# VectorE block transposes for p, score tiles of 256 columns, and V loaded in runs of eight keys per partition

## The chip, the cores and the metric

The kernel runs on one core of one Trainium2 chip. The metric is the device time of one execution in microseconds. Of seven executions of the kernel before in one set of rounds, six took 309.45 to 313.45 us; the seventh took 314.72, over 1.5% above the fastest, and such a one counts as slow. Ratios below are the mean time of one kernel's fast runs over the mean time of the fast runs of the kernel before in the same rounds, so they are not quite the ratio of the medians that are quoted beside them.

## The reference, cut to what matters

Two layers of attention over a window of 2048 cached keys, each followed by a gated feed-forward block, for 4 tokens with one query each. There are 16 query heads on 8 K/V heads of 256 dimensions. Both layers read the same caches.

```python
x = A_x                                          # 4 tokens x 448
x = x + attention(layernorm(x), k_cache, v_cache, wq, wo)
x = x + ffn(layernorm(x), w_gate, w_up, w_down)
x = x + attention(layernorm(x), k_cache, v_cache, wq, wo)
x = x + ffn(layernorm(x), w_gate, w_up, w_down)
return x
# in attention, per token and per K/V head: two queries q (2 x 256), keys K and values V (2048 x 256)
#   p = softmax(q @ K.T / 16);  o = p @ V
```

K and V of one token and head are 1 MB each, as bf16. The kernel splits each into two halves of 512 KB. Some halves are kept on the chip from the first layer for the second; all others are loaded twice.

## The kernel before

It is written as a graph of operations. The kernel's own scheduler puts them in order for the five engines from a plan (the order of heads, and offsets for the loads). These are the parts that the change and the argument touch.

```python
# loads: one DMA per half, each to all 128 partitions
ksrc = A_k_cache[t, kvh, s0:s0 + WIN, :].rearrange("(p j) d -> p (j d)", p=128)
e.dma_start(half[cell[0]][:, :], ksrc[:, 2048 * hf:2048 * hf + 2048])          # K: 8 keys, 4096 bytes a run
...
vsrc = A_v_cache[t, kvh, s0:s0 + WIN, :].rearrange("(a q g) d -> q a g d", a=4, q=128)
e.dma_start(half[cell[0]][:, :].rearrange("p (a g d) -> p a g d", a=2, g=4),
            vsrc[:, 2 * hv:2 * hv + 2, :, :])                                  # V: 4 keys, 2048 bytes a run
...
# K is turned in place by VectorE; its rows are taken as 32 groups of 32 pairs of bf16
a = half[cell[0]][:, :].bitcast(UINT32).rearrange("p (k s) -> p k s", k=32)
e.transpose(a, a)
...
# scores of a single group: a tile of 128 columns; two heads may share a group, with 256 columns
for ce in range(8):
    for hf in range(2):
        for x in range(2):
            qd = 64 * hf + 32 * x                    # 8 rows in one of the four quarters of 32 rows
            e.matmul(Sb[s_][qd:qd + 8, 0:128], lhsT=qe[...], rhs=kt[...], ...)
...
# p = exp(scores) is turned by TensorE (matmuls with selectors) and copied to bf16 by ScalarE
e.matmul(o, lhsT=praw[0:R, c0:c0 + 128], rhs=w, ...)
e.activation(pf, Yb[p_][:, 0:PW], ACT.Copy)
```

The row of q that multiplies a key is masked by the quarter of K's partitions in which the key stands. So a key's place in K's load fixes its quarter and column in the score tile. The turn of p then fixes the partition in which V's row for that key must be.

Of the kernel before, what the change touches and what calls it, by code (L numbers as in the profile page):

```python
# [5 lines left out]
ACT = mybir.ActivationFunctionType  # L6
# [7 lines left out]
B = 4  # L14
D = 448
# [11 lines left out]
KEEP_K = (6, 5, 6, 6)  # L27
KEEP_V = (5, 4, 3, 3)


KLEAD = 3.2
KTAIL = -1.1
VLAG = 0.4
SLEAD = 0.7
FR = 7.5
FRD = 10.1
WOR = -8.6
CROSS = 10
# [9 lines left out]
    ("k", 0, 0, 0): -4, ("k", 0, 0, 1): -0.5, ("k", 0, 0, 2): -1.5, ("k", 0, 0, 3): 1, ("k", 0, 0, 4): -3,  # L48
    ("k", 0, 0, 5): -0.5, ("k", 0, 0, 6): -1.5, ("k", 0, 1, 2): -0.5, ("k", 0, 1, 3): 0.5, ("k", 0, 1, 5): 2,
    ("k", 0, 1, 6): -4, ("k", 0, 1, 7): -3, ("k", 1, 0, 1): 2.5, ("k", 1, 0, 2): -3, ("k", 1, 0, 3): -0.5,  # L50
    ("k", 1, 0, 4): 2, ("k", 1, 0, 5): -0.5, ("k", 1, 0, 6): -1, ("k", 1, 1, 0): 2, ("k", 1, 1, 1): -2,
    ("k", 1, 1, 3): -4.5, ("k", 1, 1, 4): -2, ("k", 1, 1, 5): 0.5, ("k", 1, 1, 7): -3, ("k", 2, 0, 0): 2,
    ("k", 2, 0, 1): 0.5, ("k", 2, 0, 3): -1, ("k", 2, 0, 4): 2, ("k", 2, 0, 6): 2, ("k", 2, 0, 7): 0.5,
    ("k", 2, 1, 0): -2.5, ("k", 2, 1, 1): 2, ("k", 2, 1, 2): -3, ("k", 2, 1, 4): 1, ("k", 2, 1, 5): 4.5,
    ("k", 2, 1, 6): 2, ("k", 3, 0, 1): 0.5, ("k", 3, 0, 2): 3, ("k", 3, 0, 3): -1, ("k", 3, 0, 4): 1,
    ("k", 3, 0, 6): 1, ("k", 3, 1, 0): 1, ("k", 3, 1, 1): 1.5, ("k", 3, 1, 2): -6, ("k", 3, 1, 4): -1,
    ("k", 3, 1, 6): 6.5, ("k", 3, 1, 7): -4, ("v", 0, 0, 2): -2, ("v", 0, 0, 3): 0.5, ("v", 0, 0, 5): -2.5,
    ("v", 0, 0, 6): 0.5, ("v", 0, 0, 7): 1.5, ("v", 0, 1, 0): 2, ("v", 0, 1, 1): -2.5, ("v", 0, 1, 2): 3,
    ("v", 0, 1, 3): -1, ("v", 0, 1, 4): -3, ("v", 0, 1, 6): -0.5, ("v", 0, 1, 7): -3, ("v", 1, 0, 0): 3,
    ("v", 1, 0, 2): 1, ("v", 1, 0, 3): 0.5, ("v", 1, 0, 4): 4, ("v", 1, 0, 5): 1.5, ("v", 1, 0, 6): 2,  # L60
    ("v", 1, 0, 7): 1, ("v", 1, 1, 1): 2, ("v", 1, 1, 2): -3, ("v", 1, 1, 3): -1, ("v", 1, 1, 5): 0.5,
    ("v", 1, 1, 6): 0.5, ("v", 1, 1, 7): 2, ("v", 2, 0, 0): 2, ("v", 2, 0, 1): -1, ("v", 2, 0, 2): 3,
    ("v", 2, 0, 4): 1, ("v", 2, 1, 1): -3.5, ("v", 2, 1, 2): -1, ("v", 2, 1, 3): 6, ("v", 2, 1, 5): -2,
    ("v", 2, 1, 6): 1.5, ("v", 3, 0, 0): 2.5, ("v", 3, 0, 2): 1, ("v", 3, 0, 3): 1, ("v", 3, 0, 4): 1.5,
    ("v", 3, 0, 7): 1.5, ("v", 3, 1, 2): -1, ("v", 3, 1, 5): 1, ("v", 3, 1, 7): 0.5,
}
PLAN = (
    "001", "003 005", "002", "007", "004 006", "000", "100 102", "106", "017", "014 016", "101+104", "012+107",
    "105 103", "207", "010", "201", "015 301", "013", "202+117", "113", "204+205", "114 200", "011", "203", "206",
    "115 111", "112", "110", "116 300", "305 210", "307", "304+213", "303", "302", "216 306", "212 217", "215 214",  # L70
    "316+313", "211", "311+314", "310+312", "315+317",
# [8 lines left out]
TARGET = 4000  # L80
WINDOW = 3.41
HOLD = 7
HOLD_MIN = 0.8
# [27 lines left out]
class Op:  # L111
    __slots__ = ("i", "eng", "dur", "rank", "emit", "deps", "succ", "nbytes", "dsem", "dval",
                 "start", "end", "pos", "waits", "inc", "val", "known", "run", "cell", "rel", "bank")

    def __init__(self, i, eng, dur, rank, emit):
        self.i, self.eng, self.dur, self.rank, self.emit = i, eng, dur, rank, emit
        self.deps = {}
        self.succ = []
        self.nbytes = 0
        self.dsem = None  # L120
        self.dval = 0
        self.cell = None
        self.rel = ()
        self.bank = ()
        self.inc = False
        self.val = 0
        self.waits = []


class Graph:  # L130
# [42 lines left out]
    def dma(self, rank, nbytes, emit, sem, r=(), w=(), run=8192, cell=None):  # L173

        o = self.op(SP, 0.05, rank, emit, r=r, w=w)
        o.run = run
        o.nbytes = nbytes
        o.cell = cell
        if cell is None:
            self._count(o, sem)  # L180
        return o

    def _count(self, o, sem):
        o.dsem = sem
        self.dcount[sem] = self.dcount.get(sem, 0) + 16
        o.dval = self.dcount[sem]


    def schedule(self, npool):
# [16 lines left out]
        pe_end = 0.0  # L206

# [15 lines left out]
        while n < len(self.ops):  # L223
# [16 lines left out]
            if o.cell is not None:  # L240

                slot = min(pool)
# [15 lines left out]
            if e == PE:  # L258
                at = pe_end
                while t - at >= FILLD + 0.02:  # L260
                    bank = None
                    if at >= FILL0 and sum(c for b, c in busy[-24:] if b > at - WINDOW) < TARGET:
# [88 lines left out]
    def emit(self, eng_name, eng, sems, dsems):  # L351
        for o in self.order[eng_name]:
# [6 lines left out]
            if o.dsem is not None:  # L359
                ins.then_inc(dsems[o.dsem], 16)  # L360
            elif o.inc:
                ins.then_inc(sems[eng_name], 1)
# [9 lines left out]
def build(nc, A_x, A_k_cache, A_v_cache, A_wq, A_wo, B_x, B_w_gate, B_w_up, B_w_down, out):  # L372
# [3 lines left out]
    with ExitStack() as es:  # L376
# [14 lines left out]
        selt = [sb(f"selt{h}", [128, 4, 12], BF16) for h in range(2)]  # L391
        sel1 = [sb(f"sel1{h}", [128, 2, 4, 2, 2], BF16) for h in range(2)]
        small = sb("small", [128, 17 + 2 * NS + 8 * NY + 2 * B], FP32)
        onesf, wrow, lomask, expo = small[:, 0:1], small[:, 1:5], small[:, 5:6], small[:, 6:11]
# [3 lines left out]
        fars = small[:, 11:14].bitcast(BF16)  # L398
        far, far1 = fars[:, 0:4].rearrange("p (P o n) -> p P o n", P=2, o=1), fars[:, 4:6].rearrange("p (o n) -> p o n", o=1)
# [5 lines left out]
        qe = [sb(f"qe{i}", [128, 2, 8, 4, 2], BF16) for i in range(NQ)]  # L405
# [11 lines left out]
        xb = wideb[:, 0:4 * B].rearrange("p (c t) -> p c t", t=B)  # L417
        hT = wideb[:, 512:576]
        qS = wideb[:, 0:128]
        praw = sb("praw", [128, 514], BF16)  # L420
        pT = [sb(f"pT{s}", [128, 4, 4, 12], BF16) for s in range(NP)]
# [27 lines left out]
        def c_fill(e):  # L449
            e.memset(onesf[:, :], 1.0)  # L450
            e.memset(expo[:, 0:1], -0.5)
            e.memset(expo[:, 1:5], -1.0)
# [15 lines left out]
        for a in range(4):  # L468
            g.op(DVE, 0.1, R0, lambda e, a=a: e.memset(qmask[32 * a:32 * a + 32, a:a + 1], DH ** -0.5), r=("qmask",),
                 w=(f"qmask{a}",))  # L470
        ivq = identb[:, :].rearrange("p (q z n) -> p q z n", q=4, n=2)
        for h in range(2):
            g.op(DVE, 0.1, R0, lambda e, h=h: e.memset(selt[h][:, :, :], 0.0), w=(f"selt{h}",))
            for P in range(2):
                for y in range(2):
                    c0 = 8 * P + 2 * y
                    g.op(DVE, 0.1, R0, lambda e, h=h, P=P, c0=c0: e.tensor_copy(
                        selt[h][:, :, c0:c0 + 2], ivq[:, 2 * P + h, 0:4, :]), r=("identb",), w=(f"selt{h}",))
# [8 lines left out]
        for P in range(2):  # L487
            g.op(DVE, 0.1, R0, lambda e, P=P: e.tensor_scalar(
                far[:, P, 0, :], nmask[:, 2 * P:2 * P + 2], negm[0][:, 1:2], FAR,
                op0=ALU.add, op1=ALU.mult), r=("rs0", "negm0"), w=("far",))  # L490
# [6 lines left out]
        ivt = identb[:, :].rearrange("p (h x z n) -> p h x z n", h=2, x=2, n=2)  # L497
        for h in range(2):
            for y in range(2):
                for x in range(2):  # L500
                    g.op(DVE, 0.1, R0, lambda e, h=h, y=y, x=x: e.tensor_copy(sel1[h][:, x, :, y, :], ivt[:, h, x, 0:4, :]),
                         r=("identb",), w=(f"sel1{h}{y}{x}",))
        for s_ in range(NS):
            g.op(DVE, 0.2, R0, lambda e, s_=s_: e.memset(Sb[s_][:, :], 0.0), w=(f"s{s_}",), bank=(f"S{s_}",))
        g.op(DVE, 0.2, R0, lambda e: e.memset(praw[:, :], 0.0), w=("praw",))
# [47 lines left out]
        def norm(t, rank, x):  # L553
# [15 lines left out]
            vec(rank, lambda e: e.tensor_copy(s[:, 12:14], Z2[:, 0:2]), ("z2",), (k + "m",), 0.14, ("Z2",))  # L569

# [7 lines left out]
            def gp(emit, r, w, dur=0.25):  # L578
                g.op(POOL, dur, rank, emit, r=r, w=w)
            gp(lambda e: e.tensor_scalar(s[:, 15:16], s[:, 12:13], s[:, 12:13], -1e-5, op0=ALU.mult, op1=ALU.add),  # L580
               (k + "m",), (k + "e",))
            gp(lambda e: e.tensor_scalar(s[:, 5:6], s[:, 13:14], s[:, 15:16], None, op0=ALU.subtract),
               (k + "m", k + "e", k + "w", k + "v"), (k + "h",))
            gp(lambda e: e.tensor_tensor(s[:, 8:9], s[:, 5:6], expo[:, 0:1], op=ALU.pow), (k + "h", "expo"), (k + "r2",), 0.58)

        def rowvec(dst, key, ts, rank):
            for i, t in enumerate(ts):
                if i == 0:
                    g.op(POOL, 0.27, rank, lambda e, t=t: e.tensor_tensor(
                        dst, rmask[:, t:t + 1], st[:, t, 8:9], op=ALU.mult), r=("rmask", f"st{t}r2"), w=(key,))  # L590
                else:
                    g.op(POOL, 0.27, rank, lambda e, t=t: e.tensor_scalar(
                        dst, rmask[:, t:t + 1], st[:, t, 8:9], dst, op0=ALU.mult, op1=ALU.add),
# [6 lines left out]
        def qproj(ts, rank):  # L600
# [3 lines left out]
            rowvec(rvec[:, 0:1], "rvq", ts, rank)  # L604
# [52 lines left out]
        def ffn_row(ts, rank):  # L657
            rowvec(rvec[:, 1:2], "rvf", ts, rank)
            g.op(POOL, 0.27, rank, lambda e: e.tensor_single_scalar(rvec[:, 2:3], rvec[:, 1:2], 0.5, op=ALU.mult),
# [506 lines left out]
```

## Time and profile before

| | before |
|---|---|
| time, median of 2 runs | 312.48 us (312.2 to 312.75) |
| bytes loaded | 107.25 MB: 94 MB in 98 loads of V and 82 of K, the rest weights |
| last bytes | about 294 us; the tail after them 19 us |
| VectorE busy | 198.1 us (63%) |

The prediction below reads this profile and shows the lines that carry the reading. In them PE is TensorE and PEld its weight loads, DVE is VectorE, ACT ScalarE, POOL GpSimd, and SPq the queue of SyncE, which issues the loads. PEclk is the clock granted to TensorE (1.00 or 9 is full). wq and wo are the weights of attention, wg, wu and wd those of the feed-forward block; `half` is a buffer for half of K or V, S a score tile. Here are only the groups that the change replaces: the line in the program, engine, operation, output and input, count, then busy us and mean ns of one, then the engine's idle time ahead of them and what ended it.

```profile
L853 DVE STREAM_TRANSPOSE half<-half 128x1024 uint32<-128x1024 uint32 x82 | 100.3, 1230 | 3.3 <-DMA half<-in_A_k_cache_dram 3.0
...
L883 PE MATMUL S<-half,qe 128*8 128x128 bf16 x1472 | 30.6, 222 | 7.7 <-issue 3.6
...
L907 DVE TENSOR_REDUCE tiny<-S 104x1 bf16<-104x128 f32 (+1 forms) x55 | 16.8, 306 | 22.8 <-PE S L883 17.5
...
L929 ACT ACTIVATE praw<-S,small 104x128 bf16<-104x128 f32 x46 | 16.8, 365 | 55.5 <-DVE small L921 54.7
...
L951 ACT ACTIVATE pT<-Y 128x64 bf16<-128x64 f32 (+1 forms) x55 | 13.2, 240 | 20.7 <-PE Y L943 17.6
```

K's transposes (L853) are half of VectorE's work, and stay. The score matmuls (L883), the row maximum (L907) and the exponential (L929) work on 128 columns in a single group. The ScalarE copy of the turned p (L951) goes.

### The profile page before, as it was taken

How to read it: one execution, taken by the hardware profiler on the slowest of the kernel's cores; microseconds unless marked ns; L12 is line 12 of the kernel's file. 1: busy time of each engine (PE TensorE's matmuls, PEld its weight loads, DVE VectorE, ACT ScalarE, POOL GpSimd, SP SyncE). 2: the span in 40 equal slices, each digit the busy share in tenths (PEclk: the TensorE clock that was granted, in tenths of full speed). 3: DMA queues.
4: the chain of work that ended last, by engine and by line, in shares of the span. 5: the costliest groups of instructions: out<-in, count | busy, mean ns of one | idle time of the engine just before them, and what ended most of it. 6: DMA issues, size and time to landing. Idle time of an engine off the chain costs nothing.

```text
span 313.2 us, 11054 instructions
## 1 busy us (share of the span) xinstructions
PE 255.0 (81%) x4814; PEld 129.5 (41%) x4814; DVE 198.1 (63%) x627; ACT 68.1 (22%) x196; POOL 87.1 (28%) x236
## 2 busy tenths in 40 slices
PE   4788777869598867898988785988969779888996
PEld 1323323424123543264444252544435444445563
DVE  8527945845114995559778565699776656585532
ACT  0030010303003121143322032203403231423310
POOL 1521011303202322134342031441505133332530
PEclk9999999999959997799999997589999986999995
DMA  7999999999999999999999999779999998999500
GB/s 275 317 394 401 403 401 393 397 391 346 271 387 343 306 409 393 386 340 383 397 400 394 398 395 393 281 254 374 383 334 369 391 394 314 300 387 390 206 2 3
DMA packets 45024, 107.25 MB, mean 342 GB/s; under 512 B 3240, under 2 KB 8880, under 8 KB 44592
## 3 DMA queue, kind: packets, MB, share of 16 engines
q1 hardware_dynamic: 44976, 106.55, 92.9%
q8 instruction: 38, 0.62, 0.8%
q14 instruction: 10, 0.08, 0.1%
HBM read 106.53 MB, written 0.00 MB: 340 GB/s over the span
## 4 chain that ended last, share of the span: by engine, by line
PE 37%; DMA 26%; DVE 15%; SPq 14%; issue 4%; ACT 3%; POOL 1%; DVEq 0%; ACTq 0%
DMA half<-in_A_v_cache_dram 13%; DMA half<-in_A_k_cache_dram 9%; DVE half L853 7%; PE Y L973 7%; PE A L1098 7%; SPq L848 6%; SPq L527 6%; PE S L883 5%; DMA wu_sb<-in_B_w_up_dram 4%; SPq L861 3%; PE A L1026 2%; DVE oh L990 2%; PE Z L617 2%; PE Y L943 2%; PE Y L996 1%
## 5 line engine op out<-in xcount | busy, mean ns | idle before, releaser
L853 DVE STREAM_TRANSPOSE half<-half 128x1024 uint32<-128x1024 uint32 x82 | 100.3, 1230 | 3.3 <-DMA half<-in_A_k_cache_dram 3.0
L1098 PE MATMUL A<-identb,small 128*128 128x512 bf16 x249 | 83.1, 435 | 0.0
L986 POOL TENSOR_TENSOR small<-small 128x2 f32<-128x2 f32 (+1 forms) x55 | 41.3, 753 | 62.1 <-DVE small L964 59.6
L973 PE MATMUL Y<-half,pT 128*4 128x256 bf16 (+1 forms) x1024 | 46.4, 283 | 10.7 <-DMA half<-in_A_v_cache_dram 6.5
L900 POOL TENSOR_TENSOR qe<-qc,tiny 128x64 bf16<-128x64 bf16 x64 | 18.3, 293 | 83.0 <-PE S L883 61.6
L988 ACT ACTIVATE oh<-Y 128x256 bf16<-128x256 f32 x55 | 21.1, 384 | 83.0 <-PE Y L973 71.9
L990 DVE SCALAR_TENSOR_TENSOR oh<-oh,small,Y 128x256 bf16<-128x256 bf16 x55 | 25.9, 470 | 19.0 <-ACT oh L988 18.5
L883 PE MATMUL S<-half,qe 128*8 128x128 bf16 x1472 | 30.6, 222 | 7.7 <-issue 3.6
L1098 PEld LDWEIGHTS A<-identb,small 128*128 128x128 bf16 x249 | 22.8, 109 | 20.7 <-issue 12.0
L907 DVE TENSOR_REDUCE tiny<-S 104x1 bf16<-104x128 f32 (+1 forms) x55 | 16.8, 306 | 22.8 <-PE S L883 17.5
L883 PEld LDWEIGHTS S<-half,qe 128*8 128x8 bf16 x1472 | 21.8, 85 | 17.1 <-DVE half L853 5.9
L929 ACT ACTIVATE praw<-S,small 104x128 bf16<-104x128 f32 x46 | 16.8, 365 | 55.5 <-DVE small L921 54.7
L973 PEld LDWEIGHTS Y<-half,pT 128*4 128x4 bf16 (+1 forms) x1024 | 18.6, 83 | 21.4 <-DMA half<-in_A_v_cache_dram 11.7
L1026 PE MATMUL A<-wo_sb,oT 128*4 128x448 bf16 x208 | 17.8, 358 | 2.5 <-DVE oT L1006 2.1
L951 ACT ACTIVATE pT<-Y 128x64 bf16<-128x64 f32 (+1 forms) x55 | 13.2, 240 | 20.7 <-PE Y L943 17.6
L996 PE MATMUL Y<-tiny,oh 128*128 128x2 bf16 (+1 forms) x110 | 11.0, 170 | 5.9 <-DVE oh L990 5.1
L912 PE MATMUL S<-small,identb 104*104 104x32 bf16 x55 | 11.2, 214 | 5.7 <-DVE tiny L907 4.9
L580 POOL TENSOR_SCALAR st<-st 128x1 f32<-128x1 f32 x16 | 4.3, 266 | 41.4 <-DVE st L569 41.3
L921 DVE TENSOR_REDUCE small<-S 104x1 f32<-104x32 f32 x55 | 9.0, 177 | 9.4 <-PE S L915 9.2
L943 PE MATMUL Y<-sel,praw 104*128 104x32 bf16 x184 | 12.1, 180 | 2.0 <-ACT praw L929 2.0
L773 ACT ACTIVATE wide<-A 128x448 bf16<-128x448 f32 x14 | 7.6, 544 | 27.6 <-PE A L707 15.8
L895 PE MATMUL S<-half,qe 128*8 128x256 bf16 x288 | 9.9, 274 | 4.2 <-DVE half L853 3.0
(137 smaller groups left out, 296.5 us busy)
## 6 DMA issues: line engine op xcount, KB each, us to landing
half<-in_A_v_cache_dram SPq DMA_DIRECT2D x98, 512.0 KB, 8.9
half<-in_A_k_cache_dram SPq DMA_DIRECT2D x82, 512.0 KB, 8.3
wo_sb<-in_A_wo_dram SPq DMA_DIRECT2D x8, 448.0 KB, 13.3
wq_sb<-in_A_wq_dram SPq DMA_DIRECT2D x3, 1024.0 KB, 6.9
wd_sb<-in_B_w_down_dram SPq DMA_DIRECT2D x1, 1568.0 KB, 15.2
wg_sb<-in_B_w_gate_dram SPq DMA_DIRECT2D x2, 672.0 KB, 12.7
wu_sb<-in_B_w_up_dram SPq DMA_DIRECT2D x2, 672.0 KB, 13.0
wq_sb<-in_A_wq_dram SPq DMA_DIRECT2D x2, 256.0 KB, 11.4
```

What stands on the lines that cost most here:

```text
L527: g.dma(rank, nbytes, lambda e: e.dma_start(dst, src), f"w{nw[0]}", w=key if isinstance(key, tuple) else (key,), run=run)
L848: g.dma((pp - KLEAD if pp <= LAST1 else pp + KTAIL) + OFF.get(("k", t, layer, kvh), 0), 1 << 19, lambda e, cell=cell, hf=hf, ksrc=ksrc: e. ...
L853: return e.transpose(a, a)
L883: last = e.matmul(Sb[s_][qd:qd + 8, 0:128], lhsT=qe[q_][:, 0, ce, :, :].rearrange("p a n -> p (a n)"), rhs=kt[:, ce // 2, ce % 2, 2 * x:2 ...
L900: g.op(POOL, 0.25, pos - SLEAD - 1, lambda e, P=P, t=t, kvh=kvh: e.tensor_tensor(qe[q_][:, P, :, :, :], qc[t][:, kvh, :, :].unsqueeze(2).b ...
L943: last = e.matmul(o, lhsT=praw[0:R, c0:c0 + 128], rhs=w, start=(gg == 0 and h == 0), stop=False, skip_group_check=True)
L973: last = e.matmul(Yb[p_][32 * gg:32 * gg + M, 256:512], lhsT=pT[pt][:, gg, 2 * hv + a, 4 * P:4 * P + M] if n == 2 else p1[:, gg % 2, gg // ...
L986: g.op(POOL, 0.69, pos, lambda e: e.tensor_tensor(ri[p_][:, 0:2 * n], rs[p_][:, 0:2 * n], expo[:, 1:1 + 2 * n], op=ALU.pow), r=(f"rs{p_}", ...
L988: g.op(SCA, 0.34, pos, lambda e: e.activation(oh[:, :], Yb[p_][:, 256:512], ACT.Copy), r=(f"y{p_}",), w=("oh",), bank=(f"Y{p_}",))
L990: g.op(DVE, 0.43, pos, lambda e: e.scalar_tensor_tensor(out=oh[:, :], in0=oh[:, :], scalar=lomask[:, 0:1], in1=Yb[p_][:, 256:512], op0=ALU ...
L1026: last = e.matmul(Ab[32 * k:32 * k + B, 0:D], lhsT=oT[oi][:, k % 2, k // 2, :], rhs=wo_sb[:, 4 * kvh + k, :], start=False, stop=False, ski ...
L1098: g.filler = lambda b: lambda e: e.matmul(fbank[b][:, 0:512], lhsT=zero[:, 0:1].broadcast_to([128, 128]), rhs=identb[:, :].unsqueeze(1).br ...
```

## The change

Its intent: the code takes VectorE's transpose to turn each block of 32x32 by itself, so that it can turn p directly if the keys lie so that each quarter of partitions stays in its quarter. (That is what the program assumes.) This takes the turning off TensorE and ScalarE. It also lets V come in with eight neighbouring keys per partition, 4096 bytes in one run in place of two of 2048. The price in the code is that the rows of one half of V no longer follow each other at one step over all 128 partitions: the lower 64 partitions take one block of 64 rows, the upper 64 a block that starts 128 rows later. So the half is loaded by two DMAs.

```diff
-ksrc = A_k_cache[...].rearrange("(p j) d -> p (j d)", p=128)         # half hf: 8 of each 16 keys
+ksrc = A_k_cache[...].rearrange("(h p j) d -> h p (j d)", h=2, p=128) # half hf: 1024 keys in a row
-vsrc = A_v_cache[...].rearrange("(a q g) d -> q a g d", a=4, q=128)
-    e.dma_start(half[cell[0]][:, :]..., vsrc[:, 2 * hv:2 * hv + 2, :, :])
+vsrc = A_v_cache[...].rearrange("(h b s j) d -> h b s (j d)", h=2, b=2, s=64)
+    [e.dma_start(half[cell[0]][64 * h:64 * h + 64, :], vsrc[h, hv]) for h in range(2)]
 ... scores: every group has one head and 256 columns
-        e.matmul(Sb[s_][qd:qd + 8, 0:128], ...)
+        e.matmul(Sb[s_][qd:qd + 8, 0:256], ...)
 ... p
-g.op(PE, ..., turn, ...)                      # 4 or 8 matmuls with selectors
-g.op(SCA, ..., e.activation(pf, Yb[p_][:, 0:PW], ACT.Copy), ...)
+g.op(DVE, 0.21, pos, lambda e: e.transpose(pT[pt]...bitcast(UINT32), praw...bitcast(UINT32)), ...)
 ... small edits: the norm's powers as one GpSimd operation on three columns; the last token's output
     taken straight from the sum, its copy split over two engines; a denser filler at the end
 ... KEEP_K, KEEP_V, PLAN, OFF and the leads: all new (V of two heads fewer is kept on the chip)
```

## The prediction

> **What bounds the kernel now.** I read the busy table and the 40 slices first, then the DMA queue, then windows of the trace, and last the end of the chain of waits.
>
> ```profile
> PE 255.0 (81%) x4814; PEld 129.5 (41%) x4814; DVE 198.1 (63%) x627; ACT 68.1 (22%) x196; POOL 87.1 (28%) x236
> DMA  7999999999999999999999999779999998999500
> GB/s 275 317 394 401 403 401 393 397 391 346 271 387 343 306 409 393 386 340 383 397 400 394 398 395 393 281 254 374 383 334 369 391 394 314 300 387 390 206 2 3
> q1 hardware_dynamic: 44976, 106.55, 92.9%
> half<-in_A_v_cache_dram SPq DMA_DIRECT2D x98, 512.0 KB, 8.9
> half<-in_A_k_cache_dram SPq DMA_DIRECT2D x82, 512.0 KB, 8.3
> ```
>
> The DMA row is 9 from 8 us to 290 us: the loads fill the span. TensorE's 81% is not a bound, because L1098 (83 us of it) is filler [...]. K and V are 180 loads of 512 KB, 94 of the 107 MB. A load lands 8 to 9 us after its issue, so several are queued. So the time is bytes over rate, plus places where the queue starves, plus a tail after the last byte.
>
> The rate has three values. First a stretch of V alone (packets of about 2 KB), then one of K alone (4 KB):
>
> ```profile
> DMA packets 1189, 2.32 MB, mean 386 GB/s; under 512 B 65, under 2 KB 65, under 8 KB 1188
> ...
> DMA packets 573, 2.05 MB, mean 410 GB/s; under 512 B 64, under 2 KB 80, under 8 KB 573
> ```
>
> Other pure stretches give 386 to 392 for V and 405 to 412 for K, with the engines busy in both; I use 388 and 408. The third value is at 10.5 to 12.5 us, where the last quarter of wq comes in as two loads of 64 partitions each, with rows of 4096 bytes:
>
> ```profile
> DMA packets 135, 0.43 MB, mean 217 GB/s; under 512 B 25, under 2 KB 34, under 8 KB 134
> ## 3 DMA queue, kind: packets, MB, share of 16 engines
> q1 hardware_dynamic: 135, 0.43, 102.8%
> ```
>
> The engines are as busy as elsewhere, at half the rate. The only other 64-partition loads, the remainders of wg and wu, stand in the two other slow stretches of a full queue (76.5 to 80 and 82 to 86 us), below. The next lines are a starving queue and the tail; the columns are PE, PEld, DVE, ACT, POOL, the granted clock, DMA share, GB/s:
>
> ```profile
> 76.50:80.00 3.50, 2.64 (x40) 1.35 (x40) 1.20 (x10) 0.00 (x0) 1.76 (x5) 1.00 1.05 227
> 82.00:86.00 4.00, 1.56 (x17) 0.47 (x14) 0.69 (x1) 0.11 (x1) 0.00 (x0) 1.00 1.10 238
> 195.00:200.00 5.00, 4.70 (x74) 2.33 (x78) 3.20 (x15) 0.86 (x3) 1.61 (x6) 0.50 0.67 259
> 205.00:210.00 5.00, 4.32 (x120) 2.41 (x119) 4.45 (x7) 0.69 (x1) 2.74 (x8) 0.95 0.60 200
> 305.00:310.00 5.00, 5.00 (x100) 3.06 (x98) 1.15 (x8) 0.11 (x1) 0.00 (x0) 0.50 0.02 3
> ```
>
> DMA share 0.67 and 0.60 means that loads wait for buffers that DVE and PE have not freed. The last bytes come at about 294 us; 19 us of tail follow, the last of it at a granted clock of 0.50.
>
> [...] wq's two halves are neighbours in the queue and do not overlap into a full rate. No stretch of this trace shows a long row of such pairs. [...]
>
> **The change part by part.**
>
> *V loads.* Each 512 KB half of V becomes two loads of 64 partitions, first 0 to 63, then 64 to 127, with 4096-byte rows in place of 2048. The instruction counts of the changed program give 204 of them, so 102 halves against 98 (fewer V halves are kept for the second layer); K stays at 82. V bytes go from 98 x 0.524 = 51.4 MB to 53.5 MB.
> If the pairs run at K's rate: 51.4 MB at 388 GB/s is 132.4 us, 53.5 MB at 408 is 131.1 us: 1.3 us saved. The longer rows give 6.7 us and the four extra halves take back 5.3.
> If they run at wq's rate: 53.5 MB at 217 is 246.5 us: 114 us lost, all on the path.
>
> *Scores.* Two heads are no longer packed in a group: 64 groups in place of 46 single and 9 double. A group is 32 matmuls of 256 columns. The timeline has 0.56 us for a single group of 128 columns and 1.04 for 256, so PE goes from 46 x 0.56 + 9 x 1.04 = 35 us to 64 x 1.04 = 67. The extra 31 us take the place of filler (282 filler matmuls become 216), beside the DMA.
>
> *Turning p.* Out: 256 matmuls (L943, 15.4 us) and 55 ScalarE copies of pT (L951, 13.2 us). In: 64 DVE transposes of 128x128 uint32. From 1230 ns for 1024 columns, I estimate 0.15 to 0.2 us each: 11 us of DVE.
>
> *Other DVE work.* The row maximum over 256 columns: 64 x 419 ns = 26.8 us against 16.8. Nine more groups of oh, minimum and sum: 9 x (470 + 177 + 180) ns = 7 us. Two small operations in each of 16 norms: 5 us. The setup of the selectors, about 3 us, goes. DVE: 198 + 11 + 10 + 7 + 5 - 3 = 228 us, 73%. ScalarE: exponentials 64 x 473 ns = 30 against 21, oh +3.5, pT -13: level. GpSimd: 64 more small multiplies of about 0.25 us and 9 more powers, less two operations per norm, about +13 us. None of them becomes the bound; a freed buffer may come later where DVE was already tight.
>
> *Schedule.* All load offsets, the order of heads and the filler target are new. Over 195 to 215, 225 to 245 and 260 to 275 us the trace moves 4.3 MB less than 395 GB/s would, 11 us worth. I allow 2 us recovered, as a guess, against the higher DVE load.
>
> *Tail.* Three fillers of 435 ns at half clock stand at about 306 us and three more at 309; the operations behind them are late by about 0.5 and 0.7 us. [...] The last residual goes straight to the output tile and its copy is split between two engines, about 0.5 us. Sum 1.5 us.
>
> With good pairs: 312.5 - 1.3 - 2 - 1.5 = 307.7 us. With wq's rate throughout: 312.5 + 114 - 3.5 = 423 us.
>
> **The rivals.**
> *A: the pairs run at full rate.* [...] Against it: all three places with such loads are slow. For it: each is a lone pair. Result 303 to 314.
> *B[...].* [...] For it: 217 GB/s at full busy share[...]. Result 380 to 425.
> *C[...].* Some V stretches are slow and K stretches are not; half of B's loss gives about 365. Result 320 to 380.
> *D: V is well but DVE or buffers take the gain back*, so that nothing is seen: 309 to 315.
>
> **Range and chances.** The measured 217 speaks for B and C, but a change retuned in such detail is probably one whose author had reason to believe in these loads, and a lone pair is not a stream. I give A and D together 0.6, B and C 0.4. Within A and D, 307.7 with some 4 us either way puts 0.25 below 306.2 us (2% faster) and 0.35 between that and 318.7. Time 312 us, the middle of a distribution with two humps; range 302 to 400.
>
> **What would show it.** V's stretches: mean rate over pure V windows at 400 or more (A), or near 217 with DMA share about 1.0 and packets of 4096 bytes taking twice K's time (B). V's time from issue to landing would rise in B. The DMA row still 9 to the end, and the last byte's time, tell the sum. The score groups should show 64 x 32 matmuls of 256 columns, the new transpose 150 to 200 ns, DVE about 228 us busy, filler down; the last windows a clock above 0.50. The prediction is wrong if V is at full rate and the span still leaves 303 to 314, or if V is slow and the span stays near 312.

Most of the tail's 1.5 us (0.5, 0.7 and 0.5 in its parts) is estimate alone. A is that the pairs run at K's rate, B that all run at wq's, C that some do; how the author thought that A or B would come about was not shown, and is cut. Three figures can be read more closely in the trace: in the two starving stretches the waits of the load queue that it names are for TensorE alone (9.0 and 6.5 us), the six fillers of the tail take 587 to 634 ns each (435 is the mean over the whole kernel), and GpSimd's small multiply (L900) takes 293 ns, not 250.

## The result, and the profile after

The changed kernel takes **436.09 us** (median of 2 runs, 436.05 to 436.13) against 312.48. The ratio is 1.395, with a 95% interval of 1.379 to 1.410. The prediction of 312.0 us with a range of 302 to 400 was wrong. The page of the changed kernel, its busy table, rows over 40 slices, queue and issues:

```profile
PE 298.6 (69%) x4816; PEld 148.4 (34%) x4816; DVE 233.4 (54%) x745; ACT 76.7 (18%) x160; POOL 98.4 (23%) x255
...
PEclk9997769559869695968779855978888596869878
DMA  7999999999999999998999997999999979968700
GB/s 308 354 251 298 388 223 278 232 268 311 267 279 253 249 291 274 334 277 205 262 245 326 259 276 194 266 347 296 254 241 281 244 208 258 246 166 202 162 2 3
...
q1 hardware_dynamic: 34640, 108.65, 92.5%
...
half<-in_A_v_cache_dram SPq DMA_DIRECT2D x204, 256.0 KB, 11.0
half<-in_A_k_cache_dram SPq DMA_DIRECT2D x82, 512.0 KB, 13.8
```

The DMA row is still nines for most of the span, but the rate row has fallen from some 390 to 400 GB/s to about 250. The DMA engines are as busy as before (92.5% of 16 engines, 92.9% before) and move far fewer bytes in that time (252 GB/s on average, 342 before). A packet shows it too: the queue's 34640 packets took 92.5% of 16 engines over 434.2 us, so 92.5% x 16 x 434.2 / 34640 = 186 ns each; the run further below that loads V to all partitions, with runs of the same length, has 138 ns. K's loads take longer from issue to landing too, 13.8 us against 8.3. That time includes the V loads ahead of them in the queue: a load of K issued between 50 and 52 us, behind eight of V (and two of wo) issued from 41.6 us on, took 19.5 us.

Windows of the same trace tell the two kinds of load apart. The columns are the stretch, its length, the busy time of PE, PEld, DVE, ACT and POOL, the granted clock, the DMA share and GB/s:

```profile
42.00:52.00 10.00, 3.31 (x16) 1.28 (x14) 5.79 (x5) 0.00 (x0) 0.00 (x0) 0.81 1.03 405
110.00:114.00 4.00, 1.47 (x7) 0.48 (x5) 0.20 (x1) 0.00 (x0) 0.00 (x0) 1.00 1.06 230
194.00:198.00 4.00, 3.64 (x52) 1.59 (x52) 1.94 (x5) 0.56 (x2) 1.24 (x3) 0.50 0.29 92
382.00:394.00 12.00, 8.53 (x116) 3.11 (x116) 8.20 (x25) 3.07 (x6) 2.28 (x6) 0.72 0.54 149
394.00:404.00 10.00, 8.87 (x247) 6.22 (x247) 6.01 (x23) 2.89 (x6) 5.21 (x17) 1.00 1.04 232
410.00:420.00 10.00, 9.25 (x153) 4.79 (x153) 4.70 (x22) 2.59 (x6) 2.81 (x4) 0.66 0.02 5
420.00:430.00 10.00, 9.97 (x229) 6.78 (x230) 4.28 (x22) 1.85 (x5) 1.64 (x3) 1.00 0.01 2
```

From 42 to 52 us K comes in, with half a megabyte of wo among its 4 MB: 405 GB/s. From 394 to 404 us there is only V, for the last transpose of K has begun at 392.3 us: 232. From 110 to 114 us it is V with the end of wd (0.2 of 0.9 MB): 230. Two of the stretches where the queue starves, 194 to 198 and 382 to 394 us, have shares of 0.29 and 0.54. After the last bytes, at 409 us, comes a tail of 25 us.

The chain of waits agrees, and names the load:

```profile
DMA 49%; PE 24%; SPq 18%; DVE 5%; issue 3%; ACT 1%; POOL 0%; DVEq 0%
DMA half<-in_A_v_cache_dram 31%; DMA half<-in_A_k_cache_dram 18%; PE S L869 9%; SPq L848 8%; SPq L514 5%; SPq L834 5%; PE Y L920 5%; DVE half L839 3%; PE A L1044 2%; PE Z L604 1%; PE A L972 1%; PE Y L942 1%; PE A L964 1%; PE Z L709 1%; PE Z
```

The groups that answer to those of before:

```profile
L839 DVE STREAM_TRANSPOSE half<-half 128x1024 uint32<-128x1024 uint32 x82 | 101.0, 1235 | 54.8 <-DMA half<-in_A_k_cache_dram 54.6
L869 PE MATMUL S<-half,qe 128*8 128x256 bf16 x2048 | 88.7, 324 | 29.2 <-DVE half L839 23.7
L920 PE MATMUL Y<-half,pT 128*4 128x256 bf16 x1024 | 55.8, 316 | 61.3 <-DMA half<-in_A_v_cache_dram 51.0
...
L899 ACT ACTIVATE praw<-S,small 104x256 bf16<-104x256 f32 x64 | 35.1, 549 | 101.2 <-DVE small L896 91.2
...
L883 DVE TENSOR_REDUCE tiny<-S 104x1 bf16<-104x256 f32 x64 | 26.6, 415 | 23.7 <-PE S L869 23.2
...
L903 DVE STREAM_TRANSPOSE pT<-praw 128x128 uint32<-128x128 uint32 x64 | 19.3, 301 | 15.3 <-PE Y L920 10.7
```

The new transpose of p (L903) takes 301 ns, the exponential (L899) 549. Neither is what the engines wait for: matmuls of p with V (L920) wait 51 us for V, the transposes of K (L839) 55 us for K. VectorE's 233.4 us are 54% of the span.

### The profile page after: what moved, and what is told of

The parts are those of the page before. It is cut to its first block, busy times and chain, and to the rows that moved or that the text cites. A ratio compares the mean times of both kernels' runs of the same rounds, so it can differ in the third digit from the quotient of the medians.

```text
span 434.2 us, 11273 instructions
## 1 busy us (share of the span) xinstructions
PE 298.6 (69%) x4816; PEld 148.4 (34%) x4816; DVE 233.4 (54%) x745; ACT 76.7 (18%) x160; POOL 98.4 (23%) x255
## 3 DMA queue, kind: packets, MB, share of 16 engines
q1 hardware_dynamic: 34640, 108.65, 92.5%
## 4 chain that ended last, share of the span: by engine, by line
DMA 49%; PE 24%; SPq 18%; DVE 5%; issue 3%; ACT 1%; POOL 0%; DVEq 0%
DMA half<-in_A_v_cache_dram 31%; DMA half<-in_A_k_cache_dram 18%; PE S L869 9%; SPq L848 8%; SPq L514 5%; SPq L834 5%; PE Y L920 5%; DVE half L839 3%; PE A L1044 2%; PE Z L604 1%; PE A L972 1%; PE Y L942 1%; PE A L964 1%; PE Z L709 1%; PE Z L1044 1%
## 5 line engine op out<-in xcount | busy, mean ns | idle before, releaser
L839 DVE STREAM_TRANSPOSE half<-half 128x1024 uint32<-128x1024 uint32 x82 | 101.0, 1235 | 54.8 <-DMA half<-in_A_k_cache_dram 54.6
L869 PE MATMUL S<-half,qe 128*8 128x256 bf16 x2048 | 88.7, 324 | 29.2 <-DVE half L839 23.7
L920 PE MATMUL Y<-half,pT 128*4 128x256 bf16 x1024 | 55.8, 316 | 61.3 <-DMA half<-in_A_v_cache_dram 51.0
L869 PEld LDWEIGHTS S<-half,qe 128*8 128x8 bf16 x2048 | 52.0, 96 | 58.0 <-DVE half L839 28.6
L876 POOL TENSOR_TENSOR qe<-qc,tiny 128x64 bf16<-128x64 bf16 x128 | 34.7, 292 | 141.5 <-PE S L869 130.5
L1044 PE MATMUL A<-identb,small 128*128 128x512 bf16 x183 | 65.4, 462 | 0.0
L932 POOL TENSOR_TENSOR small<-small 128x2 f32<-128x2 f32 x64 | 44.7, 700 | 78.5 <-DVE small L913 71.9
L899 ACT ACTIVATE praw<-S,small 104x256 bf16<-104x256 f32 x64 | 35.1, 549 | 101.2 <-DVE small L896 91.2
L920 PEld LDWEIGHTS Y<-half,pT 128*4 128x4 bf16 x1024 | 19.8, 86 | 80.8 <-DMA half<-in_A_v_cache_dram 57.8
L883 DVE TENSOR_REDUCE tiny<-S 104x1 bf16<-104x256 f32 x64 | 26.6, 415 | 23.7 <-PE S L869 23.2
L569 POOL TENSOR_TENSOR st<-st,small 128x3 f32<-128x3 f32 x16 | 13.7, 856 | 88.7 <-DVE st L559 86.8
L903 DVE STREAM_TRANSPOSE pT<-praw 128x128 uint32<-128x128 uint32 x64 | 19.3, 301 | 15.3 <-PE Y L920 10.7
L888 PE MATMUL S<-small,identb 104*104 104x32 bf16 x64 | 13.8, 227 | 4.0 <-DVE tiny L883 3.5
## 6 DMA issues: line engine op xcount, KB each, us to landing
half<-in_A_k_cache_dram SPq DMA_DIRECT2D x82, 512.0 KB, 13.8
```

The source lines that it names most:

```text
L839: return e.transpose(a, a)
L869: last = e.matmul(Sb[s_][qd:qd + 8, 0:256], lhsT=qe[q_][:, ce, 2 * z:2 * z + 2, :, :].rearrange("p a y n -> p (a y n)"), rhs=kt[:, ce // 2 ...
L876: g.op(POOL, 0.25, pos - SLEAD - 1, lambda e, y=y, t=t, kvh=kvh: e.tensor_tensor(qe[q_][:, :, :, y, :], qc[t][:, kvh, :, :].unsqueeze(2).b ...
L883: g.op(DVE, 0.36, pos, lambda e: e.tensor_reduce(pmax[s_][0:R, :], Sb[s_][0:R, 0:N], AX.X, ALU.max), r=(f"s{s_}",), w=(f"pmax{s_}",), bank ...
L899: g.op(SCA, 0.5, pos, lambda e: e.activation(praw[0:R, :, :, :].rearrange("p j r v -> p j v r"), Sb[s_][0:R, 0:256].rearrange("p (j v r) - ...
L920: last = e.matmul(Yb[p_][32 * (j % 4):32 * (j % 4) + 4, 256:512], lhsT=pT[pt][:, j // 2, 4 * hv:4 * hv + 4, j % 2], rhs=half[vss[P][hv][0] ...
```

## The experiments

The theory after the result was rival B of the prediction: loads of 64 partitions run at half the rate however many of them are queued, and nothing else matters. Its rivals: that it is the number of DMAs (204 in place of 98), that the VectorE turn of p frees buffers late, or that the new plan is at fault.

### V loaded whole, and V loaded as two whole loads

Two edits of the changed kernel's V load alone. Both put V's rows in partitions where the changed kernel does not want them, so **their attention is wrong**. They still passed the comparison with the reference: K and q have entries of about 0.05, so the scores hardly differ, p is nearly even over 2048 keys, and the tolerance doesn't see which key a weight goes with. A calculation of the same index steps on random numbers does: it is exact for the changed kernel and far off for this edit.

```diff
-vsrc = A_v_cache[...].rearrange("(h b s j) d -> h b s (j d)", h=2, b=2, s=64)
-    [e.dma_start(half[cell[0]][64 * h:64 * h + 64, :], vsrc[h, hv]) for h in range(2)]
+vsrc = A_v_cache[...].rearrange("(b p j) d -> b p (j d)", b=2, p=128)
+    [e.dma_start(half[cell[0]][:, :], vsrc[hv])]                                          # v_whole
+    [e.dma_start(half[cell[0]][:, 1024 * h:1024 * h + 1024],
+                 vsrc[hv][:, 1024 * h:1024 * h + 1024]) for h in range(2)]                # v_two_wide
```

> The changed kernel with each 512 KB half of V loaded by one load over all 128 partitions, rows of 4096 bytes as before; the keys then lie in the wrong partitions, so the result is wrong on purpose, but work, waits and bytes are the same. If the 64-partition loads cause the loss (theory 1): V stretches at 400 to 410 GB/s, span 303 to 314 us, as step A of the prediction. If the wider score tiles, the block transposes or the lower granted clock cause it (theory 2): still 400 us or more. If the four more V halves and the new order of loads cause it: 330 us or more.

> As v_whole, but each half of V in two loads of 128 partitions with rows of 2048 bytes, so that the number of loads (204), of semaphores and of issues is that of the changed kernel. Wrong result on purpose. Theory 1 (partitions reached): V at about 388 GB/s, 308 to 318 us. Theory 3 (number of loads, issue and completion cost): 400 us or more.

With V whole: 317.31 us (median of 4; 311.82 to 321.7, two of them slow; the two fast ones average 312.9), ratio 1.004 (0.993 to 1.014). With two loads of 128 partitions: 327.25 us, ratio 1.051 (1.042 to 1.060), so above the 308 to 318 us expected for theory 1, and far below the 400 for theory 3. The rate rows of the two, with queue and V's issues of the first:

```profile
GB/s 273 350 405 403 404 404 401 399 406 351 319 409 388 384 416 406 406 409 382 364 413 411 409 374 384 347 414 409 361 369 413 408 363 386 367 261 332 5 4 3
...
q1 hardware_dynamic: 33008, 108.65, 91.6%
...
half<-in_A_v_cache_dram SPq DMA_DIRECT2D x102, 512.0 KB, 8.0
```

```profile
GB/s 276 351 398 392 398 401 389 389 397 327 322 389 371 395 400 387 398 400 339 388 400 398 400 369 329 405 399 375 344 404 388 315 322 394 274 246 210 2 4 2
```

So by the fast runs 123 us of the 124 are gone when V comes whole (119 by the median of all four), with the VectorE turn, the wide score tiles, the plan and the small edits all still in. The number of DMAs is not the cause: 204 loads of V, each to all partitions, cost 14 us over 102 by the fast runs. Of that, the runs of 2048 bytes account for 6.8 us by an estimate (53.5 MB at 388 against 408 GB/s); the rest was not taken apart. VectorE and the plan are not the cause either.

### The kernel before with only its V loads cut by partitions

The other way round: everything of the kernel before, with each V load cut into partitions 0 to 63 and 64 to 127. The result is right.

```diff
-e.dma_start(half[cell[0]][:, :]..., vsrc[:, 2 * hv:2 * hv + 2, :, :])
+[e.dma_start(half[cell[0]][64 * h:64 * h + 64, :]..., vsrc[64 * h:64 * h + 64, 2 * hv:2 * hv + 2, :, :]) for h in range(2)]
```

> The kernel before with nothing changed but that each V load is split into one for partitions 0 to 63 and one for 64 to 127 (rows of 2048 bytes, right result). Theory 1: V at 217 GB/s in place of 388 costs 51.4 MB x (1/217 - 1/388) = 104 us, so 410 to 435 us. Theory 2: about 312 us, as scores and turning are those of before.

It took 425.14 us in a fast and 435.84 in a slow run, against a median of 313.03 for the kernel before. The page is that of the slow one:

```profile
DMA  7999999999999999999999999879999999999800
GB/s 305 349 403 301 296 258 277 237 245 299 267 294 262 261 218 259 215 256 231 258 258 225 223 225 210 241 256 260 261 271 295 226 243 228 248 264 251 203 9 3
...
q1 hardware_dynamic: 46544, 106.56, 96.2%
```

The same picture: a full DMA row at 210 to 300 GB/s. With no other part of the change in it, the cut alone costs 112 us (a single fast run). Cause and effect are thus shown from both sides. The row also has 403 GB/s in its third slice, where the loads of K that were issued from 13 to 26 us come in, with 0.9 MB of wo among the 4.3 MB and none of V.

### The rates by themselves

Ahead of the kernel before, loads from the K cache were issued in stretches, each waited for before the next, so that nothing else was in the queue.

```diff
+10 loads of partitions 0..127; then 16 of 0..63; then 16 of 32..95;
+then 14 pairs 0..63, 64..127; then 8 triples 0..127, 0..63, 64..127          # all with rows of 4096 bytes
```

> The kernel before with five measured stretches of loads ahead of it, each drained before the next: 10 loads of 128 partitions, 16 of partitions 0 to 63, 16 of partitions 32 to 95, 14 pairs (0 to 63, then 64 to 127), and 8 triples (128 partitions, then a pair); rows of 4096 bytes throughout. Theory 1 [...]: about 405, 215, 400, 215 GB/s and for the triples about 283 (the mean of 408 and 217 by bytes) or below. If it is the number of partitions of a load that counts and not which: partitions 32 to 95 at 215 too. [...]

The windows, one of each stretch (the long ones lie inside their stretch):

```profile
9.00:11.00 2.00, 0.00 (x0) 0.00 (x0) 0.00 (x0) 0.00 (x0) 0.00 (x0) 1.00 1.02 412
20.00:36.00 16.00, 0.00 (x0) 0.00 (x0) 0.00 (x0) 0.00 (x0) 0.00 (x0) 1.00 1.04 208
49.00:51.00 2.00, 0.00 (x0) 0.00 (x0) 0.00 (x0) 0.00 (x0) 0.00 (x0) 1.00 1.01 402
58.00:84.00 26.00, 0.00 (x0) 0.00 (x0) 0.00 (x0) 0.00 (x0) 0.00 (x0) 1.00 1.03 231
92.00:118.00 26.00, 0.00 (x0) 0.00 (x0) 0.00 (x0) 0.00 (x0) 0.00 (x0) 1.00 1.03 262
```

This is one run. All 128 partitions: 412 GB/s. The lower 64: 208. Partitions 32 to 95: 402 at 49 to 51 us, which is among its best. From 44 to 52 us they have 371 on average, after a slow start (283 in the stretch's first 2 us). That is still far above 208, so the count of 64 partitions as such is not the trouble. A long row of 14 pairs: 231 from beginning to end. This is the experiment that the prediction wanted: the pairs do not pull apart into a full rate. And the triples: 262, where 0.524 MB at 412 and 0.524 at 231 would give 296. So a triple takes 0.46 us longer than its parts by themselves.

Why partitions 32 to 95 come near the 412 of all 128 (371 to 402) and partitions 0 to 63 stay at half of it (208), and why the two halves of a pair do not go side by side (231), no trace of this case shows. What is measured is that it depends on which 64 partitions a load reaches. The reason that theory 1 gave is cut from the expectation for that. Its 400 for partitions 32 to 95 is about what the trace of before has for K to all partitions (408), but that these 64 would reach it no trace had shown when it was written. That a long row of pairs might come in well above 215 is cut with its reason too.

### Can the two halves be made to overlap?

The same measurement with three stretches: 14 pairs as before; 14 pairs behind four small loads, to shift the two halves of the pairs against each other; and the lower halves from SyncE's queue while the upper halves come from ScalarE's.

```diff
+(a) 14 pairs;  (b) 4 loads of 8 rows into partitions 0, 4, .. 28, then 14 pairs
+(c) SyncE: 14 loads of 0..63   at the same time   ScalarE: 14 loads of 64..127
```

> The kernel before, with three stretches of measured loads of the K cache ahead of it (each waited for before the next starts, so read from the windows of each stretch). (a) Fourteen pairs of loads of 64 partitions, 0 to 63 then 64 to 127, issued one after the other from SyncE's queue: as in the earlier run of rates, 229 to 238 GB/s by every theory. (b) The same fourteen pairs, with four small loads of 8 rows ahead [...]. [...] this stretch should begin at 217 to 240 and rise towards 350 to 408 GB/s [...]. (c) Fourteen loads of partitions 0 to 63 from SyncE's queue and fourteen of partitions 64 to 127 from ScalarE's queue at the same time. [...] the stretch moves 300 to 408 GB/s. Rival, that loads to two halves are served one after the other whatever the queue: 217 to 240 GB/s. My odds: (b) rises 0.3, (c) rises 0.5. The whole kernel takes about 312 us plus 130 to 190 us of stretches.

Without a rise, (b) was to stay at 229 to 238 GB/s.

```profile
4.00:32.00 28.00, 0.00 (x0) 0.00 (x0) 4.37 (x32) 0.00 (x0) 0.00 (x0) 1.00 1.04 230
42.00:70.00 28.00, 0.00 (x0) 0.00 (x0) 0.00 (x0) 0.00 (x0) 0.00 (x0) 1.00 1.04 232
76.00:100.00 24.00, 0.00 (x0) 0.00 (x0) 0.00 (x0) 0.00 (x0) 0.00 (x0) 1.00 1.03 268
```

(a) 230 and (b) 232: the small loads change nothing. (c) 268 over its 24 us, and up to 277 in its windows. Two queues help by a sixth to a fifth, and do not come near 400. The expected 300 to 408 did not come, so this is no way to save the change. Whether the small loads in (b) shifted anything at all, the trace does not show; that part stays open.

### The small edits alone

The kernel before with only the change's small edits: the norm's powers, the direct last output, the split copy and the denser filler at the end.

> The kernel before with all of its V loads, its score tiles and its order of loads, plus only the change's small edits: the norm's three powers as one GpSimd operation on three columns, its scales prepared on VectorE, the last token's output taken straight from the sum instead of through a copy, the last copy split between ScalarE and VectorE, and more filler matmuls once all loads are issued. The result is correct. Theory: these edits touch only the tail and work that lies beside the loads, so they are worth the 1.5 us that the prediction gave the tail and no more: ratio 0.993 to 1.000, 309 to 312.5 us on a chip where the kernel before takes 312.5. Rival: they were part of what made the changed kernel slow (the longer tail, 24.7 us against 19): ratio over 1.01, with the time between the last byte and the end over 21 us.

312.65 us (6 runs), ratio 1.0003 (0.995 to 1.005). No effect is seen, though the tail is 18.1 us in this run's profile against 19.0. The 1.5 us that the prediction gave them are not seen either; they lie at the edge of the interval.

### One load with a source in two levels

The rows that a half of V needs are two blocks of 64, 128 rows apart. A DMA's source can say that, and the destination can be the plain 128 partitions. The result is right.

```diff
-    [e.dma_start(half[cell[0]][64 * h:64 * h + 64, :], vsrc[h, hv]) for h in range(2)]
+    [e.dma_start(half[cell[0]][:, :], vsrc[:, hv])]          # source 2 x 64 x 2048, destination 128 x 2048
```

> The changed kernel with one edit: each half of V comes as one load to all 128 partitions instead of two loads of 64, with the same rows in the same partitions, so that every key stands where the changed kernel wants it and the result is right by construction. The source of the load counts rows in two levels (two blocks of 64 rows, 128 rows apart), the destination is the plain 128 partitions. Theory that the whole loss is in the 64-partition loads: the ratio to the kernel before is that of the earlier run with V loaded whole, 0.99 to 1.015, 310 to 319 us; pure V windows at 400 GB/s or more, 102 V loads, about 33000 packets. Rival, that a source in two levels is cut into two loads of 64 partitions inside, or into smaller packets: 217 to 300 GB/s in V's windows and 350 to 436 us. My odds: 0.85 for the first.

> The same kernel with V in one load per half, and besides a new plan: order of heads, offsets of loads and two more halves of K and two of V kept on the chip for the second layer, found by a search with the kernel's own schedule. It moves 107.3 MB, as the kernel before does, in place of 109.4. The result is right by construction. Theory: with the rate at 400 to 411 GB/s in both K and V, the bytes set the time, so 2.1 MB less are worth 5 us against v_nest, and the longer V rows some 4 us against the kernel before: ratio to before 0.975 to 1.0, 305 to 313 us. Rival: the gaps of a starving queue and the tail set the time as much as the bytes, and a plan found on a model keeps nothing of its gain: ratio 1.00 to 1.02, as v_nest.

1239.27 us, ratio 3.97, and with the other plan 1215.18, ratio 3.89: nobody's expectation, and four times worse than the kernel before. The rows over the span, and the queue in a stretch of 4 us at the lowest rate (500 to 504 us):

```profile
DMA  7252323413213114312243111513113112121110
GB/s 264 80 154 99 106 89 108 158 53 107 100 61 107 53 53 136 108 53 80 73 128 121 53 53 53 162 53 128 61 57 103 53 53 80 53 80 71 54 53 25
```

```profile
DMA packets 53, 0.21 MB, mean 53 GB/s; under 512 B 1, under 2 KB 1, under 8 KB 53
## 3 DMA queue, kind: packets, MB, share of 16 engines
q1 hardware_dynamic: 53, 0.21, 13.0%
```

A floor of 53 GB/s, at 13.0% of 16 engines, which is 2.1 of them on average, in a run whose chain of waits is 66% loads of V. The packets are not at fault, for 53 of them carry 0.21 MB, some 4 KB each. In `v_whole` V comes in 102 loads too, to the same 128 partitions in rows of 4096 bytes, from a source in one level, and the queue is at 91.6% over the span; here it is at 25.6%. So it is the source's shape, 2 x 64 rows in two levels, that leaves most of the engines idle. How the work is shared out among the engines, and whether the outer 2 is what sets the 2.1, these runs do not show: no other shape was tried. So the theory of bytes in the second run was not tested at all.

### Another place for the keys, so that V loads plainly

If a half of K holds keys that are also the keys of one half of V, in the same partitions, V's load becomes plain (`v_whole`'s) and right. Then both halves of K must write into all four quarters of the score tile. One matmul with 104 columns of weights does so:

```diff
-for z in range(2):                                         # 32 matmuls a group, 8 columns of weights each
-    qd = 64 * hf + 32 * z
-    e.matmul(Sb[s_][qd:qd + 8, 0:256], lhsT=qe[q_][:, ce, 2 * z:2 * z + 2, :, :]..., rhs=kt[...])
+c0 = 16 * (ce // 2) + ce % 2 + 8 * (1 - hf)                # 16 matmuls a group, 104 columns of weights each
+e.matmul(Sb[s_][0:104, 0:256], lhsT=qe[q_][:, c0:c0 + 2 * 104 - 1:2], rhs=kt[...])
```

The same index steps, calculated on random numbers, give the attention to rounding. Two more kernels have the same code and new plans, found by a search with the kernel's own schedule. The first of them loads 3.1 MB less than the kernel before.

> The changed kernel with its keys placed another way, so that each half of V is one plain load to 128 partitions with rows of 4096 bytes, counted in one level. The scores matmuls are what moves: one matmul per half of K and step of the contraction now writes all four quarters of the score tile with 104 columns of weights, where two matmuls with 8 columns each wrote one quarter, and the multiplied q is laid out so that the unused rows get finite numbers that nothing reads. That gives half as many score matmuls[...], and 128 more small GpSimd operations. A calculation of the same index steps in numpy gives the attention of the reference to rounding. The plan and the offsets of the changed kernel stay. Theory that V's load shape is the whole loss: V at 400 GB/s or more and a time near the run with V loaded whole, ratio 0.99 to 1.03, 309 to 321 us; wider score matmuls may cost PE up to 40 us of busy time in place of filler. Rival, that the wider score matmuls become the bound or delay the freeing of K's buffers: over 325 us with the DMA row well under 9 in many slices.

> The same, with a plan (order of heads, offsets of loads, which halves stay on the chip) found by a search with the kernel's own schedule. It keeps 24 halves of K pairs and 17 of V against 23 and 13, so it loads 80 halves of K and 94 of V: 91.2 MB and 12.9 MB of weights, 104.1 MB against 107.3 of the kernel before. Theory that bytes and rate set the time: 3.1 MB less at 400 GB/s are 7.8 us, the longer rows of V some 4 us: ratio 0.95 to 0.985, 297 to 308 us. Rival, that the gain is given back in gaps of the queue and in the tail, which a search on a model does not see: ratio 0.985 to 1.02.

> The same with a second plan from the search, which loads 82 halves of K and 98 of V, so 107.3 MB, just as many as the kernel before. Theory that bytes and rate set the time: only the longer rows remain, 4 us, and what of the gaps the order takes away: ratio 0.975 to 1.0, 304 to 313 us, some 3 to 8 us above v_linear_plan. If it is as fast as v_linear_plan, the order and not the bytes carry the gain.

354.39 us, ratio 1.134 (1.128 to 1.140); with the plans 340.32 and 346.06, ratios 1.087 and 1.107, where 0.95 to 1.0 was expected. All are faster than the changed kernel and slower than the kernel before. The page of the first:

```profile
PE 303.0 (85%) x3771; PEld 203.6 (57%) x3771; DVE 231.4 (65%) x747; ACT 76.6 (22%) x160; POOL 117.6 (33%) x383
...
DMA  7999999699868999976999797997999589887000
GB/s 292 347 402 404 406 402 400 259 346 331 337 237 278 360 413 410 408 273 239 367 361 385 276 350 269 332 412 268 359 402 370 171 291 329 292 256 282 2 2 4
...
PE 60%; DVE 20%; SPq 9%; DMA 4%; ACT 3%; issue 3%; POOL 1%
...
L874 PE MATMUL S<-half,qe 128*104 128x256 bf16 x1024 | 129.3, 278 | 11.4 <-DVE half L845 7.1
L874 PEld LDWEIGHTS S<-half,qe 128*104 128x104 bf16 x1024 | 114.6, 128 | 20.9 <-DVE half L845 11.3
```

The rate is back at 400 to 410 where the queue is full (slices 3 to 7), so the repair of the load works. But the DMA row now has several sixes and sevens, and the chain of waits is 60% TensorE. A group's score matmuls take 129.3 / 64 = 2.02 us. In the run with V whole the 32 narrow ones take 74.3 / 64 = 1.16. One matmul is as long in both (278 and 288 ns), but of the narrow ones, each in one quarter of the score tile, 7.9 are in work at once on average, and of the wide ones 2.2 (durations added up, over the busy time). Buffers come free later, and the loads wait for them: the issues of K and V wait 86 us for matmuls of p with V, against 70 with V whole, and 211 us against 161 for TensorE in all. This was the rival for the run. The two plans differ by 3.1 MB and 1.8% in time, in the direction that bytes would have, but neither reaches 312 us. No version that beats the kernel before was found.

## Why the prediction was wrong

**The step that failed** is the last one, "The measured 217 speaks for B and C, but a change retuned in such detail is probably one whose author had reason to believe in these loads, and a lone pair is not a stream. I give A and D together 0.6, B and C 0.4." The profile of before had the fact, and it was read rightly: 217 GB/s at a full busy share for wq's pair, 227 and 238 in the two other places with such loads, and 114 us if 217 holds throughout. An assumption about the author's reasons was weighed against it. The runs put in its place: a lone pair *is* like a stream, 231 GB/s over 26 us of pairs, and cutting V's loads of the kernel before in this way costs 112 us by itself. The range, cut at 400 although B's own sum was 423, failed with it.

Point by point:

- **B's sum** was 423 us; measured 436.1. In the profiles, the last bytes moved from 294.2 to 409.1 us, +114.9, where the sum had 114 less 2 us of recovered idle time. That is right as a total, but in part by luck, for it is made up otherwise: V alone ran at 230 instead of 217, which costs less (by 14 us over 53.5 MB), and full loads beside pairs are slowed (the triples, 262 GB/s where 296 would follow from the parts), which costs more. The profile of before had a hint of this: its slow stretch of 76.5 to 80 us moved 0.79 MB, and wg's two loads of 64 partitions are only 0.23 MB. How much of the 115 us each of these and the starving gaps take was not separated.
- **The tail** was to shrink by 1.5 us; it grew from 19.0 to 25.1 us. So B's sum has this term wrong by 7.6 us, in its sign too. The clock, 0.66 from 410 to 420 us, may be part of it. But with V whole, at a clock of 1.00 for most of it, it is 23.3 us too (last bytes at 286.7 of 310.0), and with the small edits alone 18.1. So most of it comes with what the run with V whole has and the small edits have not: the new plan, the unpaired groups with wider score tiles, the new turn of p. Which of these, no run tells.
- **A's sum**, 307.7 us for good pairs, can be held against the run with V whole. In its profile the last bytes come 7.5 us earlier than before, more than the 3.3 expected. But the longer tail takes 4.3 of it, and the timed runs show no gain: ratio 1.004 (0.993 to 1.014), which leaves out A's 307.7 / 312.5 = 0.985. So even with V at full rate no gain is seen, as rival D had it, though in the profile it is the tail that takes back more than half of the 7.5 us.
- **Turning p:** 150 to 200 ns were expected of the transpose, it took 301. An eighth of the columns does not cost an eighth of 1230 ns. The exponential took 549 ns, not 473. The score matmuls took 88.7 us, not 67 (74.3 with V whole). VectorE's 233.4 us are near the 228 of the sum (228.6 with V whole). With V whole these costs are all still there, at a ratio of 1.004, so they are not what made the 124 us.
- **The clock in the tail:** the half clock of the tail is as the prediction read it, 0.50 from 305 to 310 us. What sets it was not shown by these runs. The prediction's own line has PE busy in all of those 5 us at 0.50; with V whole PE is busy in all of the 5 us from 300 to 305 at 1.00, and in 2.6 of the 5 from 305 to 310 at 0.53. With the small edits alone the last of the 40 slices has PE busy for 5 tenths at a clock of 7 tenths, where before has 6 and 5.
- **What was said to show B** did: V at 230 to 232 GB/s at a share of about 1.0, V's way from issue to landing up (11.0 us against 8.9, with half the bytes in a load), K with a little of wo still above 400 (405).

## What to carry to other kernels

Look at which partitions a load reaches before the bytes in its runs: going from runs of 2048 to runs of 4096 bytes was worth 5% of the rate here (388 against 408 GB/s), and loads to partitions 0 to 63 alone ran at half of it (208 against 412), while 32 to 95 came to 371 to 402. Where a profile has already measured a pattern at half rate with busy engines, believe it over any reason for which the pattern might do better in bulk; a few loads ahead of the kernel measure it. And look at the queue's share of the 16 engines after every change of a DMA's shape: a tidy rewrite as one load with a source in two levels ran at 13% of them and 53 GB/s at its lowest.
